# Values products made for two units at a time, with earlier weight splits, in a fused attention and expert kernel

## The chip, the cores and the metric

The kernel runs on one core of one Trainium2 chip. The metric is the device time of one execution in microseconds (us). The profile names the engines PE (TensorE), PEld (its weight loads), DVE (VectorE), ACT (ScalarE), POOL (GpSimd) and SP (SyncE, which issues most DMAs). Each engine works through its own queue in the order in which the program was written or scheduled; the engines meet only where one needs what another made.

## The reference

Causal attention mixed with a memory readout, for 4 batches, 8 heads, 576 tokens and 64 elements, then a layer of experts in which each token goes to two of eight. All in float32.

```python
scores = scale * np.matmul(q, k.transpose(0, 1, 3, 2))        # causal mask, then
a = np.exp(scores - scores.max(-1)); a /= a.sum(-1) + 1e-09   # softmax
local = np.matmul(a, v)
mem_out = (phi(q) @ M_prev) / (phi(q) @ z_prev + 1e-6)        # phi(x) = elu(x) + 1
x = g * mem_out + (1 - g) * local                             # 2304 tokens x 512
noisy_logits = x @ w_gate + log1p(exp(x @ w_noise)) * noise
# the two best experts e of each token:
out[token] += top2_w * (np.maximum(x @ w1[e], 0) @ w2[e])     # w1: 512x1024, w2: 1024x512
```

## The kernel before

**Chunks and units.** Attention goes through 20 chunks: 4 batches of 5, of 128 tokens each but the fifth, which has 64. Chunk `i` of a batch looks at `i + 1` chunks of keys. A chunk is worked off in units of heads: the first two chunks of a batch in two units of four heads, the others in four units of two heads. That makes 64 units, numbered `u`, and each chunk begins on an even one.

**One unit** passes through these steps, each on its own engine. Scores (PE, `sc`, L550 and L559, and a mask matmul, L565 or L568); the largest score of each row, negated (DVE, `nb`, L569); the exponentials (ACT, `a`, L590); their transposition (PE, `tpa`, L608) and the copy of it to SBUF (ACT, `aT`, L609); the values products (PE, `avT`, L630). In step `u` of the main loop the program writes the exponentials of unit `u + 1`, the values products of `u - 2`, the scores of `u + 2` and the transposition of `u`. The steps of the loop that are not scores or values (`xs`) are dealt out between them.

**Around the units.** Each chunk also has its preparation: queries and keys are transposed (`tpq`, `tpk`, L436), copied (`qf`, L470, `kf`, L443) and split into a high and a low part; `phi` makes `qpT` (DVE L489, ACT L415, DVE L417), and `mem` multiplies it with the memory (PE `tpm`, L497, copied by ACT to `mm`, L500). When a chunk's values are complete, ACT copies them (`xo`, L641), PE transposes them back (`tpo`, L667), DVE scales them and adds the memory's part (`xr`, L669 and L671). Then come the steps of the router: PE transposes `xr` (`tpx`, L153), ACT and DVE split it (`xTl`, L157 and L158), PE makes the logits (`tpl`, L165), turns them (`tpL`, L171) and DVE sums them (`lg`, L173). At the end of a batch some forty small DVE instructions (L199, `M` L223) find the two experts of each token and their slots; PE counts with `pp` (L243); POOL writes the slots to DRAM (`tab_scratch`, L285, called puts here). All transpositions, `tpm` and the router's matmuls share three PSUM buffers; the scores have four.

**Weights.** The experts' weights come in slices (128 of 1024 hidden units): `w1` and `w2`, 256 KB each. `split_w` turns a slice into high and low parts: `w1h` (DVE cast, L916), `w1l` (POOL subtraction, L917), `w2h` (ACT cast, L918), `w2l` (DVE subtraction, L919). The first two slices (`w0k`, `w0q`, parts named a and b) are loaded and split during attention, into buffers of the queries and keys.

**Order.** PE's order is the order in which the steps are written: `in_turn` chains them. On DVE, ACT and POOL the scheduling layer may move instructions. `early` begins the experts' input for three tiles: POOL gathers `xw` (L843) once the puts of three batches have landed, and PE turns them (`tpm` of `xw`, L891). `experts` begins with `ha` (L954).

## Time and profile before

| what | value |
|---|---|
| median of three runs | 728.72 us (724.79 to 729.32) |
| the profiled execution | 727.49 us |
| its span, first to last instruction | 725.8 us |
| PE busy | 695.0 us, 96% of the span |
| DVE, ACT, POOL busy | 459.9, 380.6, 354.9 us |
| attention, about | 0 to 276 us |
| experts, about | 276 to 726 us |

The profiled execution's own time is 1.7 us above its span; these lie outside its first and last instruction. A busy engine is not the same as an engine that is on the path: PE counts as busy while a matmul passes through, at either level of its clock.

### The profile page before, as it was taken

How to read it: one execution, taken by the hardware profiler on the slowest of the kernel's cores; microseconds unless marked ns; L12 is line 12 of the kernel's file. 1: busy time of each engine (PE TensorE's matmuls, PEld its weight loads, DVE VectorE, ACT ScalarE, POOL GpSimd, SP SyncE). 2: the span in 40 equal slices, each digit the busy share in tenths (PEclk: the TensorE clock that was granted, in tenths of full speed). 3: DMA queues.
4: the chain of work that ended last, by engine and by line, in shares of the span. 5: the costliest groups of instructions: out<-in, count | busy, mean ns of one | idle time of the engine just before them, and what ended most of it. 6: DMA issues, size and time to landing. Idle time of an engine off the chain costs nothing. (4 is left out here: it accounts for less than half of the span.)

```text
span 725.8 us, 14477 instructions
## 1 busy us (share of the span) xinstructions
PE 695.0 (96%) x5161; PEld 601.0 (83%) x5161; DVE 459.9 (63%) x1097; ACT 380.6 (52%) x963; POOL 354.9 (49%) x378
## 2 busy tenths in 40 slices
PE   7799999999999979999999999999999999999996
PEld 5678878877887767888888889889889889889885
DVE  6667687678768797967785776455455365455312
ACT  4787878787887753534664153153153153253210
POOL 4413424732842565465534776833833743723702
PEclk9899999999999999999999999999999999999999
DMA  8464432241220045869995595674694694754401
GB/s 187 85 139 95 104 73 67 67 118 44 64 61 34 2 146 152 198 174 268 233 213 162 136 220 190 160 186 140 169 198 137 175 207 136 196 145 138 125 1 63
DMA packets 173966, 98.18 MB, mean 135 GB/s; under 512 B 112852, under 2 KB 152276, under 8 KB 173888
## 3 DMA queue, kind: packets, MB, share of 16 engines
q1 hardware_dynamic: 163424, 78.20, 43.1%
q0 software_dynamic: 10080, 18.98, 9.9%
q8 instruction: 42, 0.69, 0.4%
q14 instruction: 36, 0.29, 0.2%
q10 hardware_dynamic: 384, 0.02, 0.0%
HBM read 74.41 MB, written 22.54 MB: 134 GB/s over the span
## 5 line engine op out<-in xcount | busy, mean ns | idle before, releaser
L917 POOL TENSOR_TENSOR w1lm<-w1sm,w1hm 128x512 fp32r<-128x512 f32 x72 | 93.8, 1305 | 125.6 <-DVE w1hm L916 56.4
L967 PE MATMUL y<-w2hm,hTl 128*128 128x512 f32 (+1 forms) x310 | 122.2, 394 | 0.6 <-DVE hTl L958 0.6
L967 PE MATMUL y<-w2hm,hTh 128*128 128x512 f32 (+1 forms) x310 | 122.0, 394 | 0.0
L967 PE MATMUL y<-w2lm,hTh 128*128 128x512 f32 (+1 forms) x310 | 121.4, 392 | 0.0
L957 ACT ACTIVATE hTh<-ha 128x304 fp32r<-128x304 f32 (+2 forms) x64 | 27.2, 424 | 143.5 <-PE ha L954 138.9
L919 DVE TENSOR_TENSOR w2lm<-w2sm,w2hm 128x512 fp32r<-128x512 f32 x74 | 61.5, 830 | 55.7 <-ACT w2hm L918 55.7
L918 ACT CAST w2hm<-w2sm 128x512 fp32r<-128x512 f32 x74 | 45.7, 619 | 96.5 <-PE y L967 95.8
L590 ACT ACTIVATE a<-sc,nb 128x128 f32<-128x128 f32 (+4 forms) x160 | 83.0, 531 | 14.9 <-DVE nb L569 7.6
L569 DVE TENSOR_REDUCE nb<-sc 128x1 f32<-128x384 f32 (+4 forms) x128 | 69.0, 555 | 16.0 <-PE sc L565 10.7
L916 DVE CAST w1hm<-w1sm 128x512 fp32r<-128x512 f32 x74 | 37.2, 503 | 65.4 <-PE hb L954 45.9
L967 PEld LDWEIGHTS y<-w2hm,hTl 128*128 128x128 f32 (+1 forms) x310 | 56.5, 182 | 17.2 <-DVE hTl L958 2.0
L954 PE MATMUL hb<-xTh,w1hm 128*128 128x304 f32 (+2 forms) x224 | 68.6, 306 | 0.2 <-DVE hTl L958 0.2
L954 PE MATMUL ha<-xTl,w1hm 128*128 128x304 f32 (+2 forms) x224 | 68.2, 304 | 0.0
L954 PE MATMUL hb<-xTl,w1hm 128*128 128x304 f32 (+2 forms) x224 | 67.9, 303 | 0.0
L954 PE MATMUL ha<-xTh,w1hm 128*128 128x304 f32 (+2 forms) x224 | 67.8, 303 | 0.0
L954 PE MATMUL hb<-xTh,w1lm 128*128 128x304 f32 (+2 forms) x224 | 67.7, 302 | 0.0
L954 PE MATMUL ha<-xTh,w1lm 128*128 128x304 f32 (+2 forms) x224 | 67.6, 302 | 0.0
L967 PEld LDWEIGHTS y<-w2lm,hTh 128*128 128x128 f32 (+1 forms) x310 | 56.6, 183 | 11.5
L967 PEld LDWEIGHTS y<-w2hm,hTh 128*128 128x128 f32 (+1 forms) x310 | 56.6, 183 | 10.7
L609 ACT COPY aT<-tpa 128x512 f32<-128x512 f32 x120 | 56.7, 519 | 9.2 <-PE tpa L608 8.3
L608 PE MATMUL tpa<-identr,a 128*128 128x128 f32 x400 | 59.2, 279 | 0.7 <-ACT lt L167 0.5
L507 POOL TENSOR_TENSOR xm<-mm,mr 128x256 f32<-128x256 f32 x32 | 21.1, 663 | 77.7 <-DVE mr L506 30.2
(252 smaller groups left out, 1681.1 us busy)
## 6 DMA issues: line engine op xcount, KB each, us to landing
w1sm<-in_moe_w_dram SPq DMA_DIRECT2D x74, 256.0 KB, 3.4
w2sm<-in_moe_w_dram SPq DMA_DIRECT2D x74, 256.0 KB, 4.0
y_scratch<-o SPq DMA_DIRECT2D x21, 256.0 KB, 3.6
vt<-in_v_dram SPq DMA_DIRECT2D x16, 256.0 KB, 4.1
xall_scratch<-xr SPq DMA_DIRECT2D x16, 256.0 KB, 2.5
kn<-in_k_dram SPq DMA_DIRECT2D x15, 256.0 KB, 4.1
qn<-in_q_dram SPq DMA_DIRECT2D x15, 256.0 KB, 3.1
y_scratch<-o SPq DMA_DIRECT2D x14, 224.0 KB, 4.6
```

The costliest lines, as they stand in the source:

```text
L507: (nc.gpsimd if i < 4 else nc.vector).tensor_tensor(out=d["xm"][0:n, hs, :], in0=v_[:, :, 0:64], in1=r[0:n].to_broadcast([n, 4, 64]), op=A ...
L569: nc.vector.tensor_reduce(out=nb[:, t * nh:(t + 1) * nh], in_=cols[t] if nh == 2 else cols[t][:, 0, :], axis=AX.X, op=ALU.max, negate=True)
L590: nc.scalar.activation(a[:, o:o + w], s_, AF.Exp, bias=st["nb"][:, x_:x_ + 1], accum_out=d["den"][:, at:at + 1])
L608: nc.tensor.transpose(tp[:, x_ * P:(x_ + 1) * P], a[:, (g + x_) * P:(g + x_ + 1) * P], ident)
L609: nc.scalar.copy(aT[:, g:g + w, :].rearrange("p b t -> p (b t)"), tp[:, 0:w * P])
L916: nc.vector.tensor_copy(h1, a)
L917: R["w1l"] = lo.tensor_tensor(out=l1, in0=a, in1=h1.bitcast(F32), op=ALU.subtract)
L918: nc.scalar.copy(h2, b_)
L919: nc.vector.tensor_tensor(out=l2, in0=b_, in1=h2.bitcast(F32), op=ALU.subtract)
L954: nc.tensor.matmul(o, w_[:, c, :], xT[xi][:, c, c0_ - at:c1_ - at], start=(c == 0 and i_ == 0), stop=(c == 3 and i_ == 2))
L957: R["hh"] = nc.scalar.activation(hT[0][:, c0_:c1_], o, AF.Relu)
L967: nc.tensor.matmul(ys[t][0:b_ - a_], hT[hi][:, a_:b_], w_, start=(f == 0 and i_ == 0), stop=(f == FF // P - 1 and i_ == 2))
```

## The change

- The loop makes the values products of units `u - 3` and `u - 2` together when `u` is odd, and none when it is even. The turned exponentials `aT` get five buffers where they had four.
- The first two weight slices are loaded at the start of the last batch's third chunk (before: its fifth), and split in units 56 and 58, in its fourth chunk (before: units 61 and 62, in the fifth).
- In the first units, the two `mem` steps of the second chunk are taken out of unit 1 and put at the end of unit 2.
- In the last chunk, all the router's steps of a unit stand behind the unit's transpositions; before, all but the last stood ahead of them.

```diff
-                aT = ap_.tile([P, 8, P], F32, tag="aT", name="aT", bufs=4)
+                aT = ap_.tile([P, 8, P], F32, tag="aT", name="aT", bufs=5)
...
-                if u >= 2:
-                    ys += av(u - 2)
+                if u >= 3 and u % 2:
+                    ys += av(u - 3) + av(u - 2)
...
-                    if chunks[c] == (B - 1, 4) and u == first[c]:
+                    if chunks[c] == (B - 1, 2) and u == first[c]:
                         for f in range(2):
                             W0.append(load_w(None, 0, f, None, None, [
...
-                    if chunks[c] == (B - 1, 4) and u == first[c] + 1:
+                    if chunks[c] == (B - 1, 3) and u == first[c]:
                         xs.append(lambda: here(lambda: W0.__setitem__(0, split_w(ep, W0[0], "a", 1))))
-                    if chunks[c] == (B - 1, 4) and u == first[c] + 2:
+                    if chunks[c] == (B - 1, 3) and u == first[c] + 2:
                         xs.append(lambda: here(lambda: W0.__setitem__(1, split_w(ep, W0[1], "b", 1))))
...
-                        xs += [fills.popleft()[1] for _ in range(len(rest) if u == 0 else len(fills))]
+                        xs += [fills.popleft()[1] for _ in range(len(rest) if u == 0 else len(fills) - 2)]
+                    if u == 2:
+                        end += [fills.popleft()[1] for _ in range(2)]
...
-                    xs += pops[:-1] + (trans(u) if u > 1 else []) + pops[-1:]
+                    k_ = 0 if c == len(chunks) - 1 else max(0, len(pops) - 1)
+                    xs += pops[:k_] + (trans(u) if u > 1 else []) + pops[k_:]
```

**First place: PE in units 1 to 3.** The difference in PE's order, where lines with - stand only before, lines with + only after. `tpm` is the `mem` step of the second chunk here, `sc` of width 384 the scores of units 4 and 5, `tpa` the transpositions of unit 2.

```order
 L565 MATMUL sc<-mask,identb 128x2x128
-L497 MATMUL tpm<-mz,qpT 128x130 x4
-L630 MATMUL avT<-aT,vt_116 64x128 x4
 L559 MATMUL sc<-kT,qh 128x384 x2
...
 L608 MATMUL tpa<-identr,a 128x128 x8
-L630 MATMUL avT<-aT,vt_116 64x128 x4
+L497 MATMUL tpm<-mz,qpT 128x130 x4
+L630 MATMUL avT<-aT,vt_116 64x128 x8
 L559 MATMUL sc<-kT,qh 128x384 x2
```

The `mem` step moved behind the scores of unit 4 and the transpositions of unit 2, and the values of units 0 and 1 now follow it in one piece.

**Second place: PE in a pair of units with three chunks of keys.** Before, each unit began with its own values products; the two pieces below are the even unit and the odd one.

```order
 L667 MATMUL tpo<-identr,xo 128x128 x4
-L630 MATMUL avT<-aT,vt_116 64x128 x2
-L630 MATMUL avT<-aT,vt_117 64x128 x2
-L630 MATMUL avT<-aT,vt_118 64x128 x2
 L559 MATMUL sc<-kT,qh 128x512 x2
...
 L153 MATMUL tpx<-identr,xr 128x128 x4
+L630 MATMUL avT<-aT,vt_116 64x128 x2
+L630 MATMUL avT<-aT,vt_117 64x128 x2
+L630 MATMUL avT<-aT,vt_118 64x128 x2
 L630 MATMUL avT<-aT,vt_116 64x128 x2
```

In the even unit the scores now follow the back transposition `tpo` at once, and so does everything behind them up to `tpx`; in the odd unit the values products of two units stand in one piece.

**Third place: DVE in units 56 and 57 of the last batch.** `w1ha` and `w2la` are parts of the first weight slice, `ss`, `six`, `rows` belong to the slots of the batch before it, `nb` to the next unit's scores. The kernel after counts its lines three higher here (L919 for L916, L922 for L919).

```order
+L919 CAST w1ha<-w0k 128x512
+L199 TENSOR_REDUCE ss<-t_3831 128x5
 L199 TENSOR_REDUCE ss<-t_3832 128x5
-L199 TENSOR_REDUCE ss<-t_3833 128x5
-L226 CAST rb<-run 128x8
+L922 TENSOR_TENSOR w2la<-w0q,w2ha 128x512
+L569 TENSOR_REDUCE nb<-sc 128x1
 L199 TENSOR_TENSOR six<-ss 128x5 x2
 L199 TENSOR_TENSOR ds<-ss 128x5
 L199 COPY rows<-six 128x5
```

The split stands among the slots' instructions and ahead of `nb`. The same happens a unit pair later with the second slice:

```order
+L671 TENSOR_TENSOR xr<-xr,xm 128x512
+L919 CAST w1hb<-w0k 128x512
+L922 TENSOR_TENSOR w2lb<-w0q,w2hb 128x512
+L888 MEMSET xw 128x512
+L158 TENSOR_TENSOR xTll<-tpx,xTlh 128x512
```

It stands between the sum `xr` and the split `xTll` that the logits wait for. On POOL the first subtraction now precedes the ten puts of the batch before, and the second one follows them, ahead of the three gathers of `xw`; before, both stood behind those gathers.

## Rows read from the trace of the kernel before

**Rows 1.** Windows: length; busy PE, PEld, DVE, ACT, POOL; granted clock; DMA share; GB/s.

```profile
0.00:40.00 40.00, 32.25 (x230) 24.90 (x232) 25.67 (x63) 24.84 (x75) 19.99 (x41) 0.87 0.62 134
40.00:255.00 215.00, 206.09 (x2234) 170.92 (x2232) 158.19 (x486) 175.58 (x527) 91.78 (x105) 1.00 0.29 71
255.00:285.00 30.00, 23.35 (x238) 19.93 (x237) 24.62 (x86) 15.24 (x43) 17.39 (x19) 0.94 0.51 147
```

**Rows 2.** Waits of PE up to 280 us: total, times, longest.

```profile
PE tpm L497 <- DVE qpT L417: 4.0, 1, 4.0
PE pp L243 <- DVE xTll L158: 2.8, 1, 2.8
PE tpx L153 <- DVE M L223: 2.0, 1, 2.0
PE tpx L153 <- DVE lg L173: 1.7, 3, 0.6
PE tpl L165 <- DVE xTll L158: 1.5, 3, 0.5
PE tpx L153 <- DVE xr L671: 0.9, 3, 0.3
```

**Rows 3.** Timeline (start us, us) of the first units, PE, then ACT.

```profile
24.41 2.10 PE L497 MATMUL tpm<-mz,qpT 128*128 128x130 f32 x8 [3.97 <-DVE qpT L417]
25.68 0.38 ACT L500 COPY mm<-tpm 128x260 f32<-128x260 f32 x1 [0.50 <-PE tpm L497]
26.87 0.63 ACT L415 ACTIVATE qpT<-qpT 128x512 f32<-128x512 f32 x1
29.90 0.58 ACT L470 COPY qf<-tpq 128x512 f32<-128x512 f32 x1 [2.39 <-PE tpq L436]
30.70 1.07 ACT L609 COPY aT<-tpa 128x512 f32<-128x512 f32 x2 [0.22 <-PE tpa L608]
31.66 0.60 ACT L590 ACTIVATE a<-sc,nb 128x384 f32<-128x384 f32 x1
```

**Rows 4.** Windows view: the stretch after that wait (the granted clock is PEclk).

```profile
24.40:31.00 6.60, 6.59 (x36) 5.39 (x36) 2.80 (x10) 2.95 (x9) 2.17 (x3) 0.56 0.23 52
```

**Rows 5.** Timeline of PE around values products of four and of eight pairs.

```profile
151.13 0.66 PE L630 MATMUL avT<-aT,vt 128*64 128x128 f32 x8
151.72 0.45 PE L559 MATMUL sc<-kT,qh 64*128 64x384 f32 x2
...
163.48 1.09 PE L630 MATMUL avT<-aT,vt 128*64 128x128 f32 x16
164.51 0.44 PE L559 MATMUL sc<-kT,qh 64*128 64x384 f32 x2
```

**Rows 6.** Timeline of the last batch's fourth chunk: DVE, ACT, PE, POOL.

```profile
242.58 0.18 DVE L199 TENSOR_TENSOR rows<-wa,wb 128x10 f32<-128x10 f32 x1
...
243.38 0.69 ACT L590 ACTIVATE a<-sc,nb 128x512 f32<-128x512 f32 x1 [0.73 <-DVE nb L569]
...
245.64 0.66 PE L667 MATMUL tpo<-identr,xo 128*128 128x128 f32 x4 [0.39 <-ACT kf L443]
...
243.03 1.03 POOL L285 DMA_INDIRECT tab_scratch<-rows,six  x1 [3.10 <-DVE rows L199]
```

**Rows 7.** Timeline of the last units: DVE, POOL, and the experts' first matmul.

```profile
256.57 0.42 DVE L916 CAST w1ha<-w0k 128x512 fp32r<-128x512 f32 x1
260.87 0.63 DVE L919 TENSOR_TENSOR w2la<-w0q,w2ha 128x512 fp32r<-128x512 f32 x1
263.78 3.09 DVE L663 SCALAR_TENSOR_TENSOR ar<-d,ib 64x4 f32<-64x4 f32 x1
...
260.23 1.04 POOL L843 DMA_INDIRECT xw<-xall_scratch,tabE  x1 [4.92 <-DVE nb L569]
264.35 1.28 POOL L917 TENSOR_TENSOR w1la<-w0k,w1ha 128x512 fp32r<-128x512 f32 x1
...
276.40 0.44 PE L954 MATMUL ha<-xw,w1ha 128*128 128x384 f32 x1 [0.68 <-ACT xw L895]
```

## The prediction

> **What bounds the kernel now.** I read the stages first [rows 1]. From 40 to 255 us PE is busy for 206.09 of 215 us at the full clock: attention is a queue of PE instructions with 8.9 us of holes, and a gain there is either less PE work or fewer holes. The first 40 us and the hand-over at 255 to 285 us are different: PE idles 7.75 and 6.65 us there, and the granted clock is below full (0.87 and 0.94). Then I read PE's waits [rows 2]: three single ones of 4.0, 2.8 and 2.0 us are those of the two loose stages, and the small ones at `tpx` and `tpl` come back three times each, once a batch. The experts, 276 us onward, are written alike before and after, apart from their first two slices; they start earlier or later as a whole. So the change is worth three sums: first units, the run of attention, hand-over.
>
> **First units.** PE waits 3.97 us at the `mem` step of the second chunk, since `qpT` comes late, and behind it, in PE's order, stand the values of unit 0, the scores of unit 4 and the transposition of the next queries, all ready [rows 3]. The change moves the step behind these. What is late next? PE would come to `mem` again after the transpositions of unit 2, and there it needs a PSUM buffer: the third one back is `tpq`, which ACT frees by copying `qf`. ACT ends the exponentials of unit 3 at 25.18 (the 0.50 us idle ahead of 25.68) and then has phi (0.63), `qf` (0.58), two `aT` copies (1.07) and two `mm` copies (0.38 each) ahead of the exponentials of unit 4 [rows 3]: 25.18 + 3.04 = 28.2 us, where they began at 31.66. Hence 3.5 us, set by ACT and no longer by PE. `mem` still waits, until phi and `qf` are over at about 26.4; PE reaches it at about 24, so 2.4 us of the hole stay, but with four more groups of work done. After the old hole PE ran at a mean granted clock of 0.56 for 6.6 us [rows 4], so mostly at the 1.2 GHz level; if the shorter holes keep the clock up, up to 2.9 us more of PE time is saved (6.6 x 0.44), of which ACT's queue lets little through; if the clock still falls, the gain shrinks to about 2. I take 3.5, with 1 to 5 as its ends. DVE's and POOL's work is the same and only reordered.
>
> **The run: switches saved.** Four pairs of values matmuls keep PE 0.59 us until the scores start (151.13 to 151.72), eight keep it 1.03 (163.48 to 164.51) [rows 5]. So a pair costs 0.11 us and a group has a fixed 0.15 us: the price of going from matmuls of full width to half-width ones and on to the scores. There are 32 groups fewer. If the fixed part falls away whole, that is 4.8 us; if the scores, which use half the rows, cost as much after any other matmul, nothing. The chunks of 64 tokens score with all 128 rows, so I count the whole 0.15 for their 8 even units, and half of it for the other 24: 1.2 + 1.8 = 3.0 us.
>
> **The run: waits moved.** The even unit loses its values products, so everything up to `tpx` comes 0.59 us (four pairs) to 1.03 us (eight) sooner on PE, while DVE's chain to `xr` has not become shorter; the odd unit gets the time back, so `tpl` comes later. In the second chunk of three batches `tpx` already waits for DVE (1.7 us in 3 times), and six pairs, 0.81 us by the two prices above, will be added each time: -2.4. In the 64-token chunk `tpx` waits too (0.9 us in 3), and four pairs, 0.59, are added: -1.8. In the first chunk `tpl` waits 0.5 us before the values products of its odd unit are through (1.5 in 3, one by half); that goes: +1.5 [rows 2]. In the others `tpx` doesn't wait today; I count nothing, and return to it below. The run is then 3.0 - 2.4 - 1.8 + 1.5 = +0.3 us, with ends of -3 and +5 (the ends of the switches, with and without the new waits). The fifth `aT` buffer costs nothing: four sets are alive in an even unit, and without it the next copy would wait. The earlier loads of two slices cost nothing either: 1 MB where the DMA queues are 29% busy [rows 1].
>
> **Hand-over: what the splits cost where they go.** In unit 56 DVE gets a cast (0.42) and a subtraction (0.63) ahead of the largest scores of unit 58, and POOL a subtraction of 1.28 us [rows 7]. How POOL's and DVE's work get on together shows in the last units: DVE's `ar`, on four elements a lane, took 3.09 us, while POOL made its two subtractions, the first at 264.35 for 1.28 us [rows 7]; it ended when POOL did. I count half of POOL's time, 0.6 us, for each subtraction, since DVE's reductions run on beside POOL. So ACT, which today waits 0.73 us for DVE before the exponentials of unit 58, gets them 1.65 us later, and `tpo` of the third chunk, which already waits for ACT, is 1.6 us late [rows 6]. In unit 58 cast and subtraction stand between `xr` and the `xTll` that the logits wait for, with a `memset` that was there before: 1.05 us, and 0.35 as an estimate for ACT's cast of the same slice, now in front of `xTlh` (its twin on DVE takes 0.42): 1.4. Together -3.0 us. Bounds: 0, if DVE's holes take all, and -4.4, if each POOL subtraction blocks DVE for its whole 1.28 us (2 x 0.7 more). For that end there is a rule in the Trainium skill (SBUF — State Buffer, Who interferes with whom): a DVE instruction with two inputs in SBUF and a GpSimd instruction that reads SBUF exclude each other, and the later one waits until the other is over. The 3.09 us agree with it; DVE's reductions from PSUM, which I let run on, it leaves free too. By the rule, where an instruction with two inputs comes next each time, the chunk costs 4.4 and not 3.0.
>
> **Hand-over: what they free.** `w2la` and `w2lb` leave DVE's queue ahead of `xr`, 0.63 each: 1.3 us off the wait of 2.0. `ar` falls from 3.09 to what it takes without POOL, at most 0.2: 2.9 us off, and with it the wait of 2.8 at `pp` [rows 2, 7]. PE's clock was 0.94 in the mean [rows 1]; with smaller holes I count 0.5 us of that back. Against it: the second POOL subtraction now stands behind the puts and meets DVE's router chain (-0.6), and the puts start later, 243.03 today, when `rows` is written at 242.58, behind a POOL subtraction and DVE's split; the gathers, at 260.23 today, follow them and PE may wait for the first (-0.5) [rows 6, 7]. What is late next is DVE's chain of small router instructions ahead of `xr`, so `tpx` keeps waiting about 2 us. The transpositions that were put ahead of the router's steps fill it with 0.55 us of work that PE has to do anyway. Sum: 1.3 + 2.9 + 0.5 - 0.6 - 0.5 = +3.6, with ends of 1 and 6; the first `ha`, at 276.40, comes 0.6 us earlier by this stage alone.
>
> **The sum.** 3.5 + 0.3 - 3.0 + 3.6 = 4.4 us, so 727.49 - 4.4 = 723.1 against the profiled execution's own time. That execution lies 1.2 us under the median of the runs shown; I set 723.5.
>
> **Rivals.** (a) The fourth chunk swallows the splits in DVE's holes: the -3.0 falls away and the rest of the clock comes back, some 8.5 us in all: 719. For it: DVE has 57 us without work between 40 and 255 [rows 1]. Against it: `tpo` and the logits wait there already. (b) The block moves along instead of going: POOL's subtractions stop DVE for their whole length in unit 56 and again in the last units' router chain (-0.7 more there), and puts and gathers slip by as much as the splits take (-1.4): -4.4 in the chunk and 3.6 - 0.7 - 1.4 = +1.5 in the hand-over, so 3.5 + 0.3 - 4.4 + 1.5 = 0.9: 726.6. For it: the 3.09 us. Against it: between 40 and 255 us POOL and DVE are busy side by side for 92 and 158 us [rows 1], with only the small waits of PE above. It is what the rule of the Trainium skill (SBUF — State Buffer, Who interferes with whom) would do here. (c) Slower: PE starves in even units. In 12 of the 20 chunks `tpx` does not wait today; if DVE's spare time ahead of it is shorter than the values products that leave (0.8 us on average), each of these also waits. At no spare time that is 12 x 0.8 = 9.6 us, 732.7; it decides against the kernel from 4.4 / 9.6, so once half of the spare is missing. For it: ACT is busy for 176 of 215 us, DVE for 158 [rows 1], and two of five chunks have no spare now. Against it: the other three did not wait once. (d) The move of `mem` does nothing, because PE then stands at the PSUM buffer as long as it stood at `qpT`: 1 us instead of 3.5, so 726.
>
> **How the numbers follow.** Forecast 0.42, (a) 0.24, (b) 0.14, (c) 0.11, (d) 0.09. A measurement of this kernel can tell about 1%, 7.3 us, from no change. Faster by over 1%, under 721.4: most of (a) and the lower edge of the forecast, 0.28. Slower by over 1%, over 736: the far part of (c), 0.06. The rest is 0.66. The range from 716 to 730 takes in (a) with 3 us more, (b), (d) and the near half of (c).
>
> **What would show it.** Right: the wait of 4.0 us at `tpm` shrinks to 2 to 2.5 and names ACT's `qf`; the exponentials of unit 4 start near 28; in the run `tpx` waits in the second and in the 64-token chunks grow to over 1 us each, while `tpl` waits go; `tpo` waits over 1.5 us near 246; `ar` in the hand-over is 0.2 us. Wrong: many new `tpx` waits in the other chunks (c), DVE instructions of 1 to 2 us beside both POOL subtractions (b), or no new wait in the fourth chunk and `ha` before 270 (a).

## The result, and the profile after

The changed kernel took 732.88 us (median of 20 runs, 727.68 to 734.88), the kernel before 726.93 (20 runs, 724.79 to 730.52) in the same session (kernels measured side by side make a session here): a ratio of 1.0068, with a 95% interval of 1.0054 to 1.0082. It is 0.7% slower, 5 us by the ratio and 6 between the medians, where a gain of 4.4 us (0.6%) was forecast; the forecast range ended at 730. Its profiled execution has a span of 731.5 us where before has 725.8.

Twelve of the eighteen experiments below fell into sessions in which the kernel before itself took 763 to 765 us and not 727, with long stalls. Their totals are compared with before in the same session (where two sessions are set against each other, the text says so), and the section on the hardware says what was different.

First the stages. This is the view of windows of the kernel after, the first three as in [rows 1], and two short stretches in which the clock was down. The columns are the window, its length, the busy time of PE, PEld, DVE, ACT and POOL with their numbers of instructions, the granted clock of PE, the DMA share and GB/s.

```profile
0.00:40.00 40.00, 32.82 (x260) 24.99 (x260) 25.77 (x65) 27.94 (x84) 19.77 (x41) 0.96 0.70 150
40.00:255.00 215.00, 200.42 (x2154) 167.69 (x2152) 155.73 (x479) 171.37 (x514) 92.22 (x102) 0.98 0.28 70
255.00:285.00 30.00, 23.66 (x254) 20.37 (x250) 19.94 (x79) 12.80 (x40) 19.00 (x21) 0.89 0.40 111
169.40:172.80 3.40, 3.40 (x28) 2.93 (x28) 0.88 (x3) 1.47 (x5) 0.61 (x1) 0.50 0.11 38
247.90:254.70 6.80, 5.80 (x31) 5.18 (x29) 5.35 (x11) 4.76 (x11) 5.19 (x6) 0.50 0.15 43
```

The run of attention, 40 to 255 us, was at the full clock before, with PE busy for 206.09 us [rows 1]. Now PE is busy for 200.42, so 5.7 us more of it are holes or moved work, and the clock is 0.98: it stood at the 1.2 GHz level twice.

The view of waits of PE up to 290 us, against [rows 2]. The columns are the waiting instruction, what released it, the sum, the number of times and the longest.

```profile
PE tpx L153 <- DVE xr L671: 4.9, 4, 2.8
PE tpm L497 <- ACT qf L470: 2.6, 1, 2.6
PE tpx L153 <- DVE lg L173: 2.2, 4, 0.6
PE tpo L667 <- ACT kf L443: 2.1, 3, 1.6
PE tpL L171 <- ACT lt L167: 1.9, 4, 0.6
PE tpa L608 <- DVE xr L669: 1.6, 3, 0.6
PE tpa L608 <- ACT lt L167: 1.3, 3, 0.5
PE tpx L153 <- ACT qf L470: 1.0, 3, 0.4
```

The wait for `qpT` (4.0) is gone and one of 2.6 for ACT's `qf` is there; the one at `pp` (2.8) is gone, and in the hand-over `tpx` waits 2.8 where it waited 2.0. New are waits that come three or four times, once a batch: `tpL`, `tpa` (for two releasers) and a second kind at `tpx`. Where they stand is seen in the timeline of PE. These are the third batch's, in the step of the third chunk's third unit (`tpL` is still the first chunk's there, `tpo` and `tpx` are the second's), the waiting rows and the one behind them:

```profile
166.51 0.33 PE L171 MATMUL tpL<-identr,lt 128*128 128x128 f32 x1 [0.58 <-ACT lt L167]
167.39 0.66 PE L608 MATMUL tpa<-identr,a 128*128 128x128 f32 x4 [0.55 <-DVE xr L669]
168.88 0.68 PE L153 MATMUL tpx<-identr,xr 128*128 128x128 f32 x4 [0.56 <-DVE lg L173]
169.50 2.83 PE L630 MATMUL avT<-aT,vt 128*64 128x128 f32 x24
```

Three waits of 0.55 us stand in a row, and right behind them the values products of two units run at the 1.2 GHz level (the window from 169.4): 24 matmuls in 2.83 us. The releasers tell the reason: `tpl`, `tpo`, `tpm`, `tpL`, two `tpa` and `tpx` follow one another in three PSUM buffers, so each gets the buffer of the third one back. `tpL` waits until ACT has read `tpl` (`lt`, which is also what it transposes), the first `tpa` until DVE has read `tpo` (its `xr`), and `tpx` until DVE has read `tpL` (its `lg`). In the kernel before, the six pairs of values products (12 matmuls, 0.88 us) stood between `tpo` and the scores and gave DVE and ACT that time; only the last of the three waits was there.

The last batch's third and fourth chunk, the rows that answer to [rows 6], from the timeline of all engines:

```profile
242.25 1.28 POOL L920 TENSOR_TENSOR w1la<-w0k,w1ha 128x512 fp32r<-128x512 f32 x1 [1.71 <-DVE w1ha L919]
242.38 1.69 DVE L922 TENSOR_TENSOR w2la<-w0q,w2ha 128x512 fp32r<-128x512 f32 x1
244.00 0.68 DVE L569 TENSOR_REDUCE nb<-sc 128x1 f32<-128x512 f32 x1
244.71 0.69 ACT L590 ACTIVATE a<-sc,nb 128x512 f32<-128x512 f32 x1 [1.10 <-DVE nb L569]
246.65 1.03 POOL L285 DMA_INDIRECT tab_scratch<-rows,six  x1 [3.12 <-DVE rows L199]
247.69 0.97 PE L667 MATMUL tpo<-identr,xo 128*128 128x128 f32 x4 [1.57 <-ACT kf L443]
251.09 1.09 PE L153 MATMUL tpx<-identr,xr 128*128 128x128 f32 x4 [1.00 <-DVE xr L671]
259.26 1.30 POOL L920 TENSOR_TENSOR w1lb<-w0k,w1hb 128x512 fp32r<-128x512 f32 x1
```

DVE's `w2la` takes 1.69 us beside POOL's `w1la`, where it took 0.63 [rows 7]; `nb`, the exponentials, `xo` and `tpo` follow late, as forecast (a `tpo` wait of over 1.5 us near 246). Then PE runs at the 1.2 GHz level from 247.9 to 254.7. The puts begin at 246.65 (before: 243.03).

In the hand-over, against [rows 7]:

```profile
270.02 0.63 PE L153 MATMUL tpx<-identr,xr 128*128 128x128 f32 x4 [2.77 <-DVE xr L671]
270.18 0.15 DVE L663 SCALAR_TENSOR_TENSOR ar<-d,ib 64x4 f32<-64x4 f32 x1
280.71 0.45 PE L957 MATMUL ha<-xw,w1ha 128*128 128x384 f32 x1 [0.67 <-ACT xw L898]
```

`ar` is 0.15 us and no longer 3.09, as forecast, but the first `ha` comes at 280.71 (before: 276.40). Behind it 1.4 us more go while PE is at half clock again; from 290 us on nothing is lost, and the end is 5.7 us late.

**Marks.** To see where the time goes I take one mark in each chunk, the start of its `tpo` on PE, and subtract the same mark of before. What a stretch loses is the difference of two such numbers. It can be read to some hundredths: in kernels that leave attention alone each stretch is within 0.05 us of before. From the third batch's second chunk to its third, for instance, before goes from 167.25 to 182.77 us and pair_only (below) from 167.82 to 186.32: 2.98 us lost.

```profile
167.25 0.60 PE L667 MATMUL tpo<-identr,xo 128*128 128x128 f32 x4
182.77 0.66 PE L667 MATMUL tpo<-identr,xo 128*128 128x128 f32 x4 [0.39 <-ACT kf L443]
```

(the timeline of PE in the kernel before), and in pair_only

```profile
167.82 0.66 PE L667 MATMUL tpo<-identr,xo 128*128 128x128 f32 x4
186.32 0.66 PE L667 MATMUL tpo<-identr,xo 128*128 128x128 f32 x4 [0.33 <-ACT kf L443]
```

Stretches in us (+ is lost, against before), each ending at the mark of the chunk named; the last column ends at the last `tpo`, in the hand-over. Kernels from sessions without the long stalls:

| kernel | third chunk, batches 1 to 4 | fourth chunk, batches 1 to 4 | 64-token, first and second chunk together, three times | hand-over |
|---|---|---|---|---|
| changed | +0.81, +1.38, +2.94, +2.80 | -1.21, +0.47, +0.48, +3.56 | -0.97, -0.90, -0.61 | -1.29 |
| pair_only | +0.83, +2.98, +2.98, +1.37 | -1.18, +0.47, +0.48, +0.59 | -0.93, -0.87, -0.60 | +1.65 |
| split_only | -0.02, +0.03, +0.02, +1.59 | +0.02, +0.03, 0.00, +1.14 | +0.02, +0.03, +0.02 | -3.95 |
| first_only | -0.01, +0.02, +0.01, +0.01 | +0.02, +0.02, +0.01, 0.00 | +0.04, +0.01, +0.02 | -0.42 |
| changed_but3 | -0.01, +0.71, +0.72, +2.29 | -0.96, +0.46, +0.47, +2.45 | -0.95, -0.88, -0.60 | -0.48 |
| first_but3_2 | -0.01, +0.71, +0.72, +0.71 | -0.95, +0.47, +0.46, +0.60 | -0.95, -0.88, -0.60 | +1.90 |

### The profile page after: what moved, and what is told of

The parts are those of the page before. It is cut to its first block, busy times and chain, and to the rows that moved or that the text cites. A ratio compares the mean times of both kernels' runs of the same rounds, so it can differ in the third digit from the quotient of the medians.

```text
span 731.5 us, 14477 instructions
## 1 busy us (share of the span) xinstructions
PE 695.8 (95%) x5161; PEld 603.4 (82%) x5161; DVE 457.7 (63%) x1097; ACT 380.5 (52%) x963; POOL 356.6 (49%) x378
## 3 DMA queue, kind: packets, MB, share of 16 engines
q0 software_dynamic: 10080, 18.98, 10.2%
## 5 line engine op out<-in xcount | busy, mean ns | idle before, releaser
L922 DVE TENSOR_TENSOR w2lm<-w2sm,w2hm 128x512 fp32r<-128x512 f32 x74 | 61.5, 831 | 55.8 <-ACT w2hm L921 55.8
L919 DVE CAST w1hm<-w1sm 128x512 fp32r<-128x512 f32 x74 | 37.2, 503 | 64.1 <-PE hb L957 45.9
```

The costliest lines, as they stand in the source:

```text
L919: nc.vector.tensor_copy(h1, a)
L922: nc.vector.tensor_tensor(out=l2, in0=b_, in1=h2.bitcast(F32), op=ALU.subtract)
```

## Experiments: each part of the change alone

Theory: each part does alone what it does in the changed kernel; the pairs bring waits and a lower clock, the splits hold DVE, the later `mem` gains. Rivals: one part is the whole loss, or parts lose only together. Four kernels, each the kernel before with one part of the diff shown ahead, all in one session (before: 727.72 us).

**first_only**, the later `mem` step:

```diff
-                        xs += [fills.popleft()[1] for _ in range(len(rest) if u == 0 else len(fills))]
+                        xs += [fills.popleft()[1] for _ in range(len(rest) if u == 0 else len(fills) - 2)]
+                    if u == 2:
+                        end += [fills.popleft()[1] for _ in range(2)]
```

> The kernel before with only the later mem step of the second chunk. The part theory (each part does what it did in the profile after: first units gain, the fourth chunk loses to the splits, the pairs give nothing net) expects 3 us less than before, with the exponentials of unit 4 at about 28.5 and the start carried through to the experts. Rival, the gain is taken back by the next wait: within 1 us of before, with the tpo marks of the run level again after 100 us.

Measured: 725.68 us, ratio 0.9984 (0.9970 to 0.9998), so 1.2 us less and not 3. The waits and the exponentials are as forecast:

```profile
26.19 1.66 PE L497 MATMUL tpm<-mz,qpT 128*128 128x130 f32 x8 [2.63 <-ACT qf L470]
...
28.22 0.59 ACT L590 ACTIVATE a<-sc,nb 128x384 f32<-128x384 f32 x1
```

(the timelines of PE and of ACT in first_only). The start of the first `tpo` tells why the gain is smaller. In ten traces with the step where it was (before, the nine others that leave it alone) it lies between 30.6 and 34.5 us, 32.8 in the mean; in ten with the step moved between 30.7 and 32.8, 31.7 in the mean. The difference is 1.1 us (with a standard error of 0.5), and the profile of before, from which the term was worked out, is the latest of its ten. That is not all: the exponentials of unit 4 begin at 29.7 in the mean of the first ten and at 27.4 in the mean of the others, 2.3 us earlier, so about half of what ACT gains is gone again when PE comes to `tpo`. What takes it was not tried.

**pair_only**, the pairs and the fifth buffer:

```diff
-                aT = ap_.tile([P, 8, P], F32, tag="aT", name="aT", bufs=4)
+                aT = ap_.tile([P, 8, P], F32, tag="aT", name="aT", bufs=5)
...
-                if u >= 2:
-                    ys += av(u - 2)
+                if u >= 3 and u % 2:
+                    ys += av(u - 3) + av(u - 2)
```

> The kernel before with only the values products of two units made together and five aT buffers. The part theory expects 0 to 3 us more than before: waits of 0.5 to 0.7 us in a row at tpx, tpL and tpa in the second chunk of each batch take what the switches give, and where they fall together the clock drops to 1.2 GHz for 3.4 us. Rival, the pairs are the whole loss: 6 us or more over before, with tpo after 213 us late by that much. Rival, the switches pay: 2 us or more under before, and then the late marks in the profile after came from the splits alone.

Measured: 732.15 us, ratio 1.0061 (1.0041 to 1.0081): 4.4 us more, between the theory's 3 and the rival's 6. The pairs by themselves are nearly the whole loss. The three waits are there as in the changed kernel, in batches 2, 3 and 4; behind those of batches 2 and 3 PE ran at half clock, behind those of batch 4 it did not. The view of windows ahead of the three waits and behind them:

```profile
166.00:170.00 4.00, 3.93 (x35) 2.73 (x33) 3.43 (x18) 1.98 (x7) 0.00 (x0) 1.00 0.00 0
173.20:176.60 3.40, 3.40 (x28) 2.80 (x27) 1.21 (x3) 1.83 (x5) 0.61 (x1) 0.51 0.21 76
```

So the third chunk loses 1.37 us with the full clock and 2.98 where it falls.

The hand-over of pair_only loses 1.65 us, that of first_but3_2 (below) 1.90, and the two traces show where. DVE's `nb`, on one element a lane, takes 2.70 and 2.76 us there; it ends when POOL's two subtractions do. Before, this block held `ar` (3.09), behind `xr` [rows 7]. Now it stands ahead of the second half of `xr`, and PE, from which the even unit's values products are gone, waits at `tpx` for 4.77 and 4.84 us (2.0 before). The timelines of DVE and PE in first_but3_2:

```profile
258.36 2.76 DVE L572 TENSOR_TENSOR nb<-nb 128x1 f32<-128x1 f32 x1
261.96 1.09 PE L153 MATMUL tpx<-identr,xr 128*128 128x128 f32 x4 [4.84 <-DVE M L223]
```

The wait of 2.8 at `pp` is gone in return, but the clock is at half for 10.2 us behind, where it was 3.4 before. This is read from the traces; no run moves the block alone.

**split_only**, loads and splits in the last batch's third and fourth chunk:

```diff
-                    if chunks[c] == (B - 1, 4) and u == first[c]:
+                    if chunks[c] == (B - 1, 2) and u == first[c]:
...
-                    if chunks[c] == (B - 1, 4) and u == first[c] + 1:
+                    if chunks[c] == (B - 1, 3) and u == first[c]:
...
-                    if chunks[c] == (B - 1, 4) and u == first[c] + 2:
+                    if chunks[c] == (B - 1, 3) and u == first[c] + 2:
```

> The kernel before with only the loads and splits of the two weight slices one and two chunks earlier. The part theory expects 3 to 6 us more than before: POOL's subtractions hold DVE, nb and the exponentials of unit 58 come 1.3 us late, tpo waits, the clock falls at 248, the puts move behind 246; ar falls from 3.09 to 0.2 us, which gives back 1 to 3. Rival, the splits lose only beside paired units, where the waits come close together: 1 to 3 us less than before, no 1.2 GHz stretch near 250. Rival of the forecast, 3.6 freed against 3.0 lost: within 1 us.

Measured: 728.62 us, ratio 1.0024 (1.0005 to 1.0043): 1.7 us more, less than the theory's 3 to 6, and not the gain of the first rival. Up to the last `tpo` the splits cost 2.7 (1.59 + 1.14) and give 3.95 back; 0.98 of it is lost again up to the first `ha`. That one stands 1.94 us ahead of before's, where the first `tpo` of the run stood 1.88 ahead, so up to `ha` the splits cost nothing on balance. PE waits twice, and the clock stays full from 244 to 251:

```profile
244.06 0.66 PE L608 MATMUL tpa<-identr,a 128*128 128x128 f32 x4 [1.01 <-DVE lg L173]
245.54 0.66 PE L667 MATMUL tpo<-identr,xo 128*128 128x128 f32 x4 [0.82 <-ACT kf L443]
```

DVE's two subtractions are the same work, one beside POOL's and one alone; the third row is a small instruction of the slots beside POOL's second subtraction, `w1lb`:

```profile
240.08 1.69 DVE L919 TENSOR_TENSOR w2la<-w0q,w2ha 128x512 fp32r<-128x512 f32 x1
...
248.79 0.69 DVE L919 TENSOR_TENSOR w2lb<-w0q,w2hb 128x512 fp32r<-128x512 f32 x1 [0.20 <-ACT w2hb L918]
256.23 1.76 DVE L199 TENSOR_TENSOR z<-z,lg 128x24 f32<-128x24 f32 x1
```

POOL's `w1la` ran from 239.95 to 241.23, and 1.69 is the 1.15 that were left of it plus 0.54 of `w2la`'s own. DVE waits for all that is left of POOL's subtraction, and not for half of it as the prediction took; the Trainium skill's rule (SBUF — State Buffer, Who interferes with whom), that a DVE instruction with two SBUF inputs and a GpSimd one that reads SBUF exclude each other, agrees with these rows. `z` took 0.18 before; POOL's `w1lb` ran from 256.63 to 257.93 and `z` ended at 257.99. Behind it the next `nb` and exponentials are late and `tpo` waits 1.15 us at 261.31, which is the fourth chunk's 1.14. Where the 1.7 us of the total come from is not settled. In the profiled execution, 3.2 us longer than that of before, the loss lies among the experts: PE waits 1.74 us at 337.94 for ACT, which had waited 6.63 for the transposing DMA (4.50 before), and the clock falls there.

```profile
334.97 1.41 ACT L1065 COPY xf<-trn 128x512 uint16<-128x512 uint16 x2 [6.63 <-DMA trn<-pl]
337.94 0.50 PE L967 MATMUL y<-w2hm,hTh 128*128 128x512 f32 x1 [1.74 <-ACT hTh L957]
```

changed_but3 (below) has the same hole with 1.06 us, the changed kernel has none, and no_split_2, without the early splits, loses 3 us in the same stretch: it is not tied to the splits alone.

**drain_only**, the order in the last chunk:

```diff
-                    xs += pops[:-1] + (trans(u) if u > 1 else []) + pops[-1:]
+                    k_ = 0 if c == len(chunks) - 1 else max(0, len(pops) - 1)
+                    xs += pops[:k_] + (trans(u) if u > 1 else []) + pops[k_:]
```

> The kernel before with only the other order in the last chunk: the router's transpositions behind those of the exponentials. All theories but one expect no difference (within 1 us). Rival, the order is what made the 2.77 us wait at tpx in the hand-over and the slow clock at the experts' start: 2 us or more over before.

Measured: 727.28 us, ratio 1.0005 (0.9991 to 1.0020). No difference. The four parts add up: -0.0016 + 0.0061 + 0.0024 + 0.0005 = 0.0074, where the whole change has 0.0068.

## Experiments: which pairs, and what about them

Theory A: the three waits in the third chunk, and the clock behind them, are the loss. Theory B (the prediction's rival c): PE starves a little in every even unit. Theory C: five buffers, or where they lie, cost time. These sessions fell among the long stalls, which stand in the fourth chunks of batches 2 to 4 and in the hand-over; the marks of the chunks between them are clean, as before_2 shows.

**pair_but3** and, in another session, **pair_but3_2**: pair_only, but the third chunk's products unit by unit.

```diff
-                if u >= 3 and u % 2:
+                if u >= 2 and chunks[units[u - 2][0]][1] == 2:
+                    ys += av(u - 2)
+                elif u >= 3 and u % 2:
                     ys += av(u - 3) + av(u - 2)
+                if u >= 3 and u % 2:
...
```

> The kernel before with pairs everywhere but in the third chunk of each batch, whose values products stay unit by unit. Theory A (the three waits in a row, 1.7 us together, and the 1.2 GHz stretch behind them are the loss of the pairs): the waits at tpL, tpa and tpx in the third chunk are those of before again, no half clock between 40 and 255 us, 1 to 3 us less than before. Theory B (PE starves a little in every even unit): two thirds of the loss of pairs everywhere stay, 2 us or more over before. Theory C (five buffers of aT, or where they lie, cost time): the whole 4 us stay.

> The kernel of pair_but3 beside a chip on which before takes its 727 us. Chunk by chunk, pair_but3 showed 0.7 us lost in the third chunk where pair_only lost 1.4 to 2.9, no half clock in the run outside the long stalls, and the other chunks as in pair_only: 2 to 4 us less than pair_only, so within 1.5 us of before. If pairs cost everywhere, 2 us or more over before.

Measured: 756.63 us against 763.57, ratio 0.9914 (0.9887 to 0.9941); then 759.85 against 765.41, 0.9928 (0.9907 to 0.9949). The third chunk loses 0.72 us in batches 2 to 4 and nothing in the first; two of the three waits are left, and the clock behind them is full, in all six places:

```profile
176.08 0.66 PE L608 MATMUL tpa<-identr,a 128*128 128x128 f32 x4 [0.53 <-DVE xr L669]
177.58 0.66 PE L153 MATMUL tpx<-identr,xr 128*128 128x128 f32 x4 [0.56 <-DVE lg L173]
...
174.00:184.00 10.00, 8.91 (x90) 6.74 (x89) 7.22 (x25) 7.97 (x24) 1.22 (x2) 1.00 0.19 54
```

(timeline of PE, and the window, of pair_but3_2). Theory A's prediction of the total ("1 to 3 us less than before") came out too small among the stalls, and the second run did not get the session without stalls that its expectation asked for. Theories B and C, which both had these kernels 2 to 4 us slower than before, fall; first_but3_2 (below), with five buffers and no stalls, is level with before.

**pair_only_2**, pair_only once more, and **before_2**, the kernel before, both among the stalls.

> The kernel before itself, profiled beside the chip with the long stalls. If the stalls belong to the chip and not to the edits, its trace has them at the same three places (behind 120, 190 and 260 us), 8 us each, and the chunks between them take the same time as in the first profile of before, within 0.1 us.

> Pairs everywhere, beside the same chip. If the third chunk's pairs are the loss here too, 4 us or more over pair_but3_2, with the third chunk 1.4 us late at full clock and 3.0 with the half clock; the long stalls can hide or add up to 3 us. If the pairs cost nothing beside the stalls, the time of pair_but3_2.

Measured: before_2 has the stalls, +8.2, +10.1 and +11.2 us at the three places, and every other stretch of the run within 0.02 us of the first profile of before. pair_only_2 took 762.21 us against 763.07, ratio 0.9992 (0.9965 to 1.0018); its third chunks lose 1.36, 1.39 and, with the half clock, 2.93. Against pair_but3_2, from another session, the third chunk's pairs cost 0.0064 (with the two intervals put together, 0.003 to 0.010), 4.9 us of 765.

**pair_fill** and **pair_fill_2**: pair_only with four idle matmuls ahead of each of the three waiting steps, in batches 2 to 4.

```diff
+    def fill(tp):
+        for _ in range(4):
+            nc.tensor.matmul(tp[:, 0:256], warm[:, 0:P], warm[:, 0:256], start=True, stop=True)
...
+            if b and i == 1:
+                fill(tp)
...
+            if b and i == 0:
+                fill(tp)
...
+                    if u > 16 and u % 16 == 6 and g == 0:
+                        fill(tp)
```

> Pairs everywhere as in pair_only, and in the third chunk of batches 2 to 4 four idle matmuls of 256 columns ahead of each of the three waiting steps (tpL, tpa, tpx), some 0.43 us in each wait of 0.55 us; they write a bank that the step overwrites. Theory A says that the waits themselves stay and only the clock is mended: no half clock between 40 and 255 us, 2 to 4 us less than pair_only. If the waits alone are the loss, the same time as pair_only, and up to 1 us more where a filler is longer than its wait.

> The kernel of pair_fill beside such a chip. If the clock makes half of the loss of the pairs: no half clock between 40 and 255 us, the third chunk 1.8 us late each time where pair_only is 1.4 late at full and 2.9 at half clock, 1 to 3 us less than pair_only. If the waits alone count: the time of pair_only, 4 us over before.

Measured: 761.64 us against 763.57, ratio 0.9976 (0.9951 to 1.0000), and 764.02 against 765.41, 0.9986 (0.9966 to 1.0007): not to be told from pair_only_2, where theory A expected 2 to 4 us less. In the traces the clock stays full behind all six, where it fell at four of the twelve such places of pair_only, pair_only_2, no_split and no_split_2. At one in three, six in a row stay full by luck in one case of eleven (0.67 to the sixth power is 0.09), so it is not shown that the fillers keep the clock up. And the third chunk loses 1.73 to 1.77 us each time, 0.39 more than the bare waits cost at the full clock (the timeline of PE in pair_fill_2):

```profile
175.27 0.60 PE L148 MATMUL tpL<-warm 128*128 128x256 bf16 x4 [0.58 <-ACT lt L173]
176.15 0.60 PE L148 MATMUL tpa<-warm 128*128 128x256 bf16 x4 [0.17 <-DVE xr L679]
177.64 0.60 PE L148 MATMUL tpx<-warm 128*128 128x256 bf16 x4 [0.18 <-DVE lg L181]
```

The fillers write the same buffer as the step, and they wait for the same releasers. So what PE waits for is the PSUM buffer and not the data: a filler can't stand in that wait, it can only come behind it. If the fillers do prevent a fall in one case of three, 1.6 us each, they gain 0.5 us on average and cost 0.4.

**first_pair014**: the later `mem`, and pairs in the first, second and 64-token chunks only (the lines of the pairs, against pair_only).

```diff
+                if u >= 2 and chunks[units[u - 2][0]][1] in (2, 3):
+                    ys += av(u - 2)
+                elif u >= 3 and u % 2:
                     ys += av(u - 3) + av(u - 2)
+                if u >= 3 and u % 2:
...
```

> The kernel before with the later mem step and with pairs in the first, second and 64-token chunks alone; the third and fourth chunks go unit by unit. In the trace of pair_only the chunks with pairs gave back 0.8 us a batch in the first and second chunks and lost 1.4 to 2.9 us in the third and 0.5 in the fourth. If that holds chunk by chunk, 3 to 4 us less than before (1.2 of it from the first units), no half clock between 40 and 255 us. If what is saved in one chunk only brings the next wait, the 1.2 us of the first units alone.

Measured: 762.70 us against 765.41, ratio 0.9978 (0.9959 to 0.9997), 1.7 us less. The third chunk loses 0.72 us here too, with no pairs of its own: what is left there is made by the pairs of the chunks ahead of it, whose `tpo`, `xr` and `tpx` come into it. What is saved in one chunk brings a wait in the next, as the expectation's second case has it.

## Experiments: splits beside pairs

**no_split** and **no_split_2**: the changed kernel with loads and splits back where they were. **changed_2**: the changed kernel. All among the stalls.

> The changed kernel with the two loads and splits back in the last chunk, as before. If the parts add up as they did alone (first units -1.2, pairs +4.4, last chunk's order +0.4, splits +1.8), 3 us over before and 2 us under the changed kernel, with the half clock of the third chunks still there and none at 248. Rival, the splits lose only beside paired units (fourth chunk: 6 us late by 260 us): within 1 us of before, 4 us or more under the changed kernel.

> The kernel of no_split beside such a chip. Sum of the parts alone: 3 us over before and 2 under the changed kernel. If the splits lose mainly beside paired units: within 1 us of before, with the fourth chunk's 6 us gone and no half clock at 248.

> The changed kernel, beside the same chip. Against no_split_2 it tells what the splits cost next to pairs: 2 us more if they add up as alone, 4 us more or beyond if they lose mainly beside paired units; the fourth chunk of the last batch 2.8 and 3.6 us late as in its first profile, and the hand-over gives back 1.3 or more.

Measured: 761.81 us against 763.57, ratio 0.9967 (0.9942 to 0.9992); 763.42 against 765.41, 0.9975 (0.9952 to 0.9999); and the changed kernel 757.31 against 763.07, 0.9923 (0.9901 to 0.9945). All three expectations fail in the total: among the stalls the splits do not cost 2 to 4 us, they save 3 to 4 (from two sessions), and the changed kernel is the faster one. In the marks the last batch's third chunk of changed_2 loses the same 2.80 us; what differs is behind it: its fourth chunk and hand-over together lose 8.3 us, where no_split_2 loses 12.5, pair_only_2 13.1 and before_2 16.8. The splits are out of the hand-over, which has a stall there; how the two are bound up was not tried.

**no_pair**: the changed kernel without pairs, four buffers.

> The changed kernel with the values products unit by unit and four buffers again: later mem, earlier splits, the other order in the last chunk. If the pairs are what costs, within 1.5 us of before on either side (-1.2 +1.8 +0.4), no half clock between 40 and 240 us and about 2.7 us lost in the fourth chunk that the hand-over gives back. If the splits are the loss, 3 us or more over before.

Measured, among the stalls: 748.22 us against 763.57, ratio 0.9796 (0.9768 to 0.9825), from five runs. Its marks agree with the theory where no stall is (third chunks 0.00, 0.02 and 0.01, then 1.59 with the split), and the hand-over gives back 2.93; that and a smaller stall in the fourth chunk (5.68 for 11.18) make the total. It says little of a session without stalls.

**changed_but3**: the changed kernel with the third chunk's products unit by unit, in a session without stalls (before: 727.37), and **first_but3_2** beside it, the later `mem` with the same pairs; the latter had been run among the stalls as **first_but3**.

> The changed kernel with the third chunk's values products unit by unit again. If the pairs of the third chunk are what makes the splits cost more than alone, the third chunk of the last batch is about 2.3 us late (0.7 from what is left of the pairs, 1.6 from the split) instead of 2.8, with the full clock at 248; the third chunks of the other batches 0.0 and 0.7 late instead of 0.8 and 1.4; in all 2 to 5 us under the changed kernel beside the same chip. If the splits bring the half clock at 248 by themselves, the third and fourth chunk of the last batch stay 6 us late together, and 1 to 2 us under the changed kernel.

> The kernel of first_but3, beside the same chip as changed_but3: the two tell what the earlier splits and the last chunk's order are worth when the third chunk has no pairs. By the marks the splits lose 2.7 us in the last batch's third and fourth chunks and give 4 back in the hand-over, so changed_but3 is 0 to 2 us faster than this. Without the long stalls, 2 to 4 us less than before; beside them, 6 to 8 less, as first measured there.

> The kernel before with the later mem step and pairs everywhere but in the third chunk of each batch; splits and last chunk as before. From the marks of the traces: the third chunk 0.7 us late in three batches, the 64-token chunk and the first one 0.9 us a batch early, the fourth early by 1.0 in the first batch: 1.3 to 2 us less than before in the run, 1.2 to 2.4 from the first units, so 2 to 4 us less than before, with no half clock between 40 and 255 us if there are no long stalls. If the fourth chunk loses 0.5 in later batches as in pair_only, 1 to 2.5 less. Rival, pairs cost by their mere presence: 1 us or more over before.

Measured: changed_but3 728.31 us, ratio 1.0015 (1.0000 to 1.0031); first_but3_2 726.90, 1.0003 (0.9982 to 1.0023); first_but3 755.48 against 762.75, 0.9895 (0.9865 to 0.9925). So taking the pairs out of the third chunk alone removes 0.0053 of the change's 0.0068 (from another session), 3.9 of 5 us: the third chunk's pairs are the larger part of the loss, with about the same size as among the stalls, as theory A has it. But first_but3_2 is no faster than before, where 2 to 4 us were expected: the run gains 1.2 us in the first batch and the hand-over loses 1.90.

On the question of the splits neither case of the expectation holds whole. As in the first, the third chunk of the last batch is 2.29 us late, those of the other batches 0.7 or nothing, and the total is 3.9 us under the changed kernel; as in the second, the clock falls. Third and fourth chunk of the last batch lose 4.7 us together. The waits there:

```profile
242.20 0.66 PE L608 MATMUL tpa<-identr,a 128*128 128x128 f32 x4 [1.00 <-DVE lg L173]
243.68 0.80 PE L667 MATMUL tpo<-identr,xo 128*128 128x128 f32 x4 [0.82 <-ACT kf L443]
246.92 1.09 PE L153 MATMUL tpx<-identr,xr 128*128 128x128 f32 x4 [1.00 <-ACT w2hb L924]
...
244.10:250.90 6.80, 5.80 (x34) 5.10 (x33) 5.71 (x14) 4.75 (x11) 5.11 (x6) 0.50 0.16 43
```

The clock fell at 244.1, behind the first two of these waits and ahead of the third. split_only has the same two and kept the full clock. no_pair has them too, without any pairs, and there the clock fell right behind them:

```profile
262.33 0.71 PE L667 MATMUL tpo<-identr,xo 128*128 128x128 f32 x4 [0.82 <-ACT kf L443]
262.80:266.20 3.40, 3.40 (x23) 2.89 (x22) 2.00 (x4) 2.74 (x7) 2.67 (x3) 0.50 0.16 51
```

So the splits can bring the half clock by themselves, now and then: of the five executions with the earlier splits it fell here in three (the changed kernel, changed_but3, no_pair) and not in two (split_only, changed_2). A wait like the third one stands in first_but3_2 too (`tpx`, 1.11 us), with pairs in the fourth chunk and no split near. Splits and these pairs together lose 4.7 us where the sum of both is 4.0 (2.7 and 1.3); the rest fits the half clock, but no run separates it.

## Why the prediction was wrong, point by point

**The step that failed is "The run: waits moved".** In the steps of the third chunk it counted one wait a batch, `tpx` of the second chunk, 0.81 us longer, one more of 0.59 in the 64-token chunk, and nothing in the chunks that did not wait. The values products that leave an even unit are cover for more than `tpx`: each step that needs one of the three PSUM buffers had them too. Without them three waits come one after another, which cost 1.37 us a batch and not 0.81, and the fourth chunk of batches 2 and 3 loses 0.47. The sign that was named did not come: `tpx` still waits 0.56 us in the second chunk and 0.6 to 0.7 in the 64-token chunk, and not over 1 us. Added up for pair_only at the full clock, the stretches up to the fourth chunk of batch 4 lose 2.7 us (of the marks, 5.9, less 1.6 for each of two falls of the clock), where the sum had a gain of 0.3; the lower end given, -3, was about right for that much. The pairs also lose 1.65 to 1.90 us in the hand-over, which was counted apart from them: there DVE's block beside POOL stands ahead of `xr` now, and no values products of the even unit cover the wait. The two make 4.4 us, the loss of pair_only by its ratio. What was in no term is the clock: 1.6 us more each time it falls in a third chunk, none to two times in the executions traced. In the prediction the clock of the run stood at 1.00 and was only ever a gain to be had in the other stages. The profiled execution of pair_only, with two falls, is the slowest of its six.

**The sum, in the two profiled executions.** First units 3.0 us gained (3.5 forecast); the run with the splits in it 8.6 lost (0.3 - 3.0 forecast, so 2.7 lost); hand-over up to the first `ha` 1.3 gained (3.6); behind `ha` 1.4 lost (no term). That is 5.7 us lost in place of 4.4 gained.

**Switches saved** were real in kind: the 64-token, first and second chunks together give back 0.6 to 1.0 us a batch, and the first batch's fourth chunk 1.2, where nothing new waits. With the second chunk of the first batch that is 3.8 us in pair_only, against the 3.0 of this term and the 1.5 of the `tpl` waits, which went as said.

**First units**: right in mechanism (wait of 2.63 for ACT's `qf`; exponentials of unit 4 at 28.22, worked out as 28.2), mis-sized as a term: 3.5 us against 1.2 measured. It was worked out from an execution whose first units were the latest of ten, and it took ACT's gain for PE's: of 2.3 us at the exponentials 1.1 are left at `tpo`.

**Fourth chunk**: -3.0 was forecast and -2.7 measured with the splits alone, in part by luck. The first slice came on the path that was worked out and with its size (1.6 forecast, 1.59 measured), though it keeps DVE for 2.1 us and not for 1.65. For the second, 1.4 was counted at the logits, behind cast, subtraction and `memset`; that wait did not grow (0.23 us at `tpl`, as before). The 1.14 came from POOL's `w1lb`, which held DVE's `z`. Each of the two subtractions holds DVE for all that is left of it, as the rule of the Trainium skill named there (SBUF — State Buffer, Who interferes with whom) has it, and not for half. In the changed kernel the two chunks lose 6.4: 2.7 of the splits, 2.0 of the pairs (1.37 and 0.59 in pair_only), and 1.7 more, in an execution whose clock stood at half there.

**Hand-over**: +3.6 forecast; with the splits alone +3.95 up to the last `tpo` and 2.97 up to the first `ha`, and `ar` at 0.15 in the changed kernel. There +1.29 is left beside the pairs, and 1.4 are lost again at half clock behind the first `ha`. Splits and hand-over together are near zero up to `ha` with the splits alone, as the two terms said (-3.0 and +3.6).

**Rivals.** (c) came nearest: new waits in even units, though in the third and fourth chunks and not everywhere, and its price was spread over 12 chunks where three waits in one place make most of it. (a) is out: the splits cost 2.7 us where they go. (b) is half true: the whole block came, but the later gathers cost PE one wait of 0.90 us in split_only (`tpm` of `xw` at 265.16) and none in the changed kernel. (d) had the size of the first units, 1 us, but not the reason: PE stands 2.6 us at the buffer, and stood 4.0 at `qpT`.

## What to carry to other kernels

Before work is moved off the place where it stands, list everything on that engine behind it that needs a buffer from a small ring: the work was cover for each of these, not just for the one that waits today. A stage at the full clock has something to lose; a few short waits one after another can cost more through the clock than through their own length, and only now and then, so one profile does not tell. A gain worked out from one profiled execution should be set against several where the stage has no steady time, and the first 35 us here have none.

## What the runs showed of the hardware

**The clock falls in some executions and not in others.** The same three waits of 0.55 us, in the same places, were followed by half clock in four of twelve cases without fillers or splits, and two such waits never in the twelve cases of pair_but3, pair_but3_2, first_but3 and first_but3_2. All else in those chunks agrees to 0.03 us. Why one execution falls and the next does not stays open. In the twenty executions of the changed kernel a longer time goes with a lower mean clock, from 727.7 us at 0.989 to 734.9 at 0.983. That fits, but 0.006 of 730 us are 4.4 of these 7.2 us at most, and first units (30.7 to 32.8 us) and experts differ between executions too, so how much of the spread is the clock is not shown.

**Two kinds of sessions.** In four of the six sessions of the experiments before took 763 to 765 us. The chip alone does not make it: one and the same took 727.72 us in the first session and 763.57 in the second. The trace of before_2 has the same chunks to 0.02 us, and stalls of 8 to 11 us in the fourth chunks of batches 2, 3 and 4, while POOL makes its ten puts, and one in the hand-over. PE, ACT and DVE stand still for some 4 us at a time, and nothing that the trace names is late: `tpx` waits for 4.04 us, with `xr` written at 120.86, for a buffer that ACT frees, and ACT for a release that the trace shows only as remote.

```profile
120.17 0.69 DVE L671 TENSOR_TENSOR xr<-xr,xm 128x512 f32<-128x512 f32 x1
126.08 0.59 ACT L470 COPY qf<-tpq 128x512 f32<-128x512 f32 x1 [4.74 <-remote]
126.72 0.66 PE L153 MATMUL tpx<-identr,xr 128*128 128x128 f32 x4 [4.04 <-ACT qf L470]
```

What makes the stalls stays open. They turn the verdict: the changed kernel is 0.7% slower without them and 0.8% faster among them (0.9923), and the marks put the difference into the last batch's fourth chunk and the hand-over. The pairs of the third chunk cost 4 to 5 us in both, each time by kernels of two sessions.
